# A new hand-written issue order for an adaptive-LayerNorm block on one core

## The chip, the core and the metric

The kernel runs on one core of a Trainium2 chip. The metric is the device time of one execution in microseconds (us). Three runs of the kernel before took 236.52, 236.69 and 236.73 us. TensorE (PE) multiplies matrices, VectorE (DVE) and ScalarE (ACT) work on elements, GpSimd (POOL) does a few small things, and SyncE (SP) issues nearly all the DMA transfers. PEld in the profile is TensorE's loading of weights.

## The reference

One token sequence x of 2048 x 512 passes through a transformer block whose two normalisations are scaled and shifted by a condition c:

```python
mod = (silu(c) @ w_mod).reshape(1, 6, 1, 512)
sa, ca, ga, sb, cb, gb = (mod[:, i] for i in range(6))
h = layernorm(x) * (1 + ca) + sa
x = x + ga * attention(h)
h = layernorm(x) * (1 + cb) + sb
x = x + gb * ((gelu(h @ w_gate) * (h @ w_up)) @ w_down)
```

The attention has 32 heads of width 16. Query s sees 8 keys only, those at s, s-2, ..., s-14, and the softmax runs over these 8. w_gate and w_up are 512 x 1792, w_down is 1792 x 512. All is bfloat16.

## The kernel before

**Segments and stages.** The 2048 tokens are four segments (sg 0 to 3) of 512. Each one passes through the same stages, and the stages of different segments are interleaved. The names below are those of the code; a number behind a name is the segment, a second one the part of it.

| stage of segment g | engine and line | what it does |
|---|---|---|
| LN1.g.st, vd, va, rs, x | DVE L430, L460, L465; POOL L471; DVE L448 | statistics by 128 rows, 1/deviation, xn = normalised x (four instructions x0 to x3) |
| LN1.g.sa, nm, sq | ACT L408, L414, L419 | the statistics of some rows on ACT instead |
| LN1.g.th (g = 0), LN1.1.t | PE L509, L484 | transposes of xn |
| LN1.g.t (g = 2, 3), LN2.g.t (g = 1, 2, 3) | SP L490 | the same as a DMA transpose |
| LN1.g.h | ACT L545, DVE L543 (g = 0); ACT or POOL L527, L525 | scale and shift: hT. For g = 0 these read the modulation mod01 |
| qph, qp.g.b.j | PE L580, L598 | q, k and v products (b = 0, 1, 2), four parts each; ACT (L618, L620, L624) copies them out |
| vst.g, V4.g.0 to 2, V4ld.g | SP L635, L644 | v goes to DRAM and comes back shifted, in four loads V; V4ld is the last of the four |
| pq.g.j, lp.g | DVE L664; PE L678 | q times the shifted k, then summed over a head by a column-tiled product |
| mx, z, e, s1, ri, p | DVE L695, L701, L711, L717, L722; ACT L706 | softmax |
| ptp.0; est, ptl (g > 0) | PE L736; SP L750, L758 | probabilities brought into v's layout |
| pv.g.j, o.g.j | DVE L771; PE L790 | probabilities times v, summed by a column-tiled product; ACT L801 copies out (oT) |
| x1p, x1, LN2 | PE L811; DVE L820; as LN1 | output projection, residual, second norm |
| g, u, gl, ub, hh | PE L844; ACT L878, L885; DVE L896 | gate and up products, gelu, their product: 14 tiles each |
| y, ot, sto | PE L856, L868; DVE L903; SP L928 | down product, residual, store |

The modulation needs products of its own: mp1 and mp0 (PE L348) for mod01 (DVE L355), mp3 and mp4 (PE L305), and mp2 and mp5 (PE L369) for ga and gb. gst and ga (SP L319, L323) send ga through DRAM to all partitions. At the head PE runs 20 products of zeros (w0 to w19, L217).

**Column-tiled products.** lp, o, ptp, mp2 and mp5 use only 32 columns of the array in an instruction and say which: `tile_position=(0, H * g)`. lp and o are eight instructions each, ptp, mp2 and mp5 sixteen. All other products use the full array. A run of column-tiled products with no full product between them is called a stretch here.

**The order.** Every stage is a Python generator (a thread) of operations. A list of thread numbers, ORDER, says which thread gives its next operation; this fixes the order of issue on each engine, and each engine's queue runs in that order:

```python
for i in ORDER:
    op = nxt[i]
    assert all(name in self.done for name in op.after), (op.fire, op.after)
    ...
    op.fn()
```

So an instruction that waits keeps back all that stands behind it on its engine. SP's queue is one too: a load that stands behind a store waits until that store has been issued. Buffers are few: one for vT (what ACT writes and vst sends), one for V, two for hT, four PSUM banks for the products q, k, v, g, u and y, and two for o and x1p.

Of the kernel before, what the change touches and what calls it, by code (L numbers as in the profile page):

```python
# [16 lines left out]
PT_DMA = (1, 2, 3)  # L17

ORDER = [
# [35 lines left out]
]  # L55


# [920 lines left out]
```

## Time and profile before

| | |
|---|---|
| runs | 236.52, 236.69, 236.73 us |
| span of the profiled execution | 234.1 us, so some 2.6 us of a run lie around it |
| TensorE's granted clock | 1.000 |
| PE busy | 230.0 us, 98% of the span |
| DVE, ACT, POOL busy | 170.4, 150.0, 18.6 us |
| DMA | 30.21 MB, mean 129 GB/s |

The page gives busy time by engine, a chain of what ended last, and groups of instructions. A row of the timeline has start, duration, engine, line, operation, output<-inputs and count; several instructions that follow one another are merged in a row. Matmuls are pipelined and overlap, so the distance from one start to the next is what counts, not the duration. An SP row says how long the issue took, not the transfer.

### The profile page before, as it was taken

To read this page: it belongs to the slowest core of one execution; us is meant where nothing else is said; L and a number is where in the kernel's file an instruction comes from. 1 tells how busy PE (TensorE), PEld (TensorE's weight loads), DVE (VectorE), ACT (ScalarE), POOL (GpSimd) and SP (SyncE) were. 2 spreads that over 40 slices of the span, in tenths; PEclk is the share of its full clock that TensorE was granted. 3 is DMA by queue.
4 is the path that set the end of the run, shared out by engine and by line. 5 is a ranking of instruction groups with operands and counts; after the bars stand their busy time and mean duration, and the time that the engine had idled before them with its cause. 6 is when DMAs were issued, how large, how long until landed. Compare 5 with 4: busy or idle time off the path is not lost.

```text
span 234.1 us, 3675 instructions
## 1 busy us (share of the span) xinstructions
PE 230.0 (98%) x1387; PEld 108.2 (46%) x1387; DVE 170.4 (73%) x240; ACT 150.0 (64%) x283; POOL 18.6 (8%) x43
## 2 busy tenths in 40 slices
PE   7999999999999999999999999999999999999995
PEld 2755455434644444444444444444444444444443
DVE  3999999999997999999799788467747421222222
ACT  4899997976997758936656492546754343666400
POOL 2612461000100000100000010000001000000000
PEclk9999999999999999999999999999999999999999
DMA  6997989999969839553102963510000411000011
GB/s 218 373 364 213 202 213 171 276 391 303 176 152 236 291 92 200 98 114 103 56 0 57 202 109 60 156 56 0 0 4 0 90 45 45 3 0 0 0 48 45
DMA packets 36265, 30.21 MB, mean 129 GB/s; under 512 B 14872, under 2 KB 34328, under 8 KB 36248
## 3 DMA queue, kind: packets, MB, share of 16 engines
q1 hardware_dynamic: 35968, 29.72, 50.6%
q10 hardware_dynamic: 280, 0.26, 0.3%
q8 instruction: 11, 0.18, 0.3%
q14 instruction: 6, 0.05, 0.1%
HBM read 22.37 MB, written 4.98 MB: 117 GB/s over the span
## 4 chain that ended last, share of the span: by engine, by line
PE 98%; DVE 0%; issue 0%
PE g_ps L844 21%; PE u_ps L844 21%; PE y_ps L856 19%; PE qkv_ps L598 17%; PE x_ps L811 6%; PE o_ps L790 3%; PE LTp L678 3%; PE warm_ps L217 3%; PE y_ps L868 1%; PE qkv_ps L580 1%; PE hTp L484 1%; PE hTp L509 0%; PE modT_ps L305 0%; PE modT_ps L348 0%; PE gR_ps L369 0%; PE PTp L736 0%
## 5 line engine op out<-in xcount | busy, mean ns | idle before, releaser
L844 PE MATMUL g_ps<-h,Wg 128*128 128x512 bf16 x224 | 57.5, 379 | 0.0
L844 PE MATMUL u_ps<-h,Wu 128*128 128x512 bf16 x224 | 57.5, 379 | 0.0
L878 ACT ACTIVATE gl<-g_ps 128x512 bf16<-128x512 f32 x56 | 33.6, 600 | 24.8 <-PE g_ps L844 23.9
L856 PE MATMUL y_ps<-Wd,hht 128*128 128x512 bf16 x210 | 46.0, 379 | 0.0
L885 ACT CAST ub<-u_ps 128x512 bf16<-128x512 f32 x56 | 32.8, 586 | 18.3 <-PE u_ps L844 18.1
L598 PE MATMUL qkv_ps<-hT,wqkv 128*128 128x512 bf16 x184 | 42.1, 380 | 0.0
L896 DVE TENSOR_TENSOR hht<-gl,ub 128x512 bf16<-128x512 bf16 x56 | 23.0, 421 | 25.3 <-ACT ub L885 25.0
L664 DVE TENSOR_TENSOR pq<-qT,kT 128x4096 bf16<-128x4096 bf16 x16 | 36.3, 2292 | 0.0
L771 DVE TENSOR_TENSOR pv<-PT,V 128x4096 bf16<-128x4096 bf16 x16 | 36.0, 2286 | 0.0
L844 PEld LDWEIGHTS <-Wg 128*128 128x128 bf16 x224 | 21.5, 98 | 27.3 <-issue 2.1
L844 PEld LDWEIGHTS <-Wu 128*128 128x128 bf16 x224 | 21.8, 98 | 26.6 <-issue 0.4
L856 PEld LDWEIGHTS <-hht 128*128 128x128 bf16 x210 | 20.5, 98 | 24.8
L598 PEld LDWEIGHTS <-wqkv 128*128 128x128 bf16 x184 | 20.1, 114 | 19.7 <-issue 3.0
L903 DVE TENSOR_TENSOR ot<-y_ps,x 128x512 bf16<-128x512 f32 x15 | 10.3, 689 | 20.2 <-PE y_ps L856 17.2
L471 POOL TENSOR_TENSOR rstd<-rstd,neghalf 128x4 f32<-128x4 f32 (+1 forms) x9 | 8.8, 980 | 154.1 <-DVE rstd L460 85.5
L527 ACT ACTIVATE h<-h,modT,scl 128x512 bf16<-128x512 bf16 x12 | 8.8, 802 | 11.6 <-DMA h<-xn 11.6
L811 PE MATMUL x_ps<-woP,oT 128*128 128x512 bf16 x64 | 15.3, 379 | 0.0
L430 DVE BATCH_NORM_STATS2 st<-x 128x6 f32<-128x512 bf16 x19 | 12.9, 680 | 3.1 <-DMA x<-in_A_x_dram 2.9
L820 DVE TENSOR_TENSOR x<-x_ps,x 128x512 bf16<-128x512 f32 x16 | 10.8, 686 | 5.0 <-PE x_ps L811 5.0
L801 ACT CAST oT<-o_ps 128x512 bf16<-128x512 f32 x16 | 8.9, 592 | 2.7 <-PE o_ps L790 2.7
L618 ACT CAST qT<-qkv_ps 128x512 bf16<-128x512 f32 x16 | 9.2, 587 | 2.2 <-PE qkv_ps L598 2.1
L620 ACT CAST kT<-qkv_ps 128x512 bf16<-128x512 f32 x16 | 9.5, 596 | 1.2 <-PE qkv_ps L598 1.2
(85 smaller groups left out, 181.5 us busy)
## 6 DMA issues: line engine op xcount, KB each, us to landing
V<-vscr SPq DMA_DIRECT2D x12, 520.0 KB, 10.4
wm<-in_w_mod_dram SPq DMA_DIRECT2D x6, 512.0 KB, 5.4
vscr<-vT SPq DMA_DIRECT2D x4, 512.0 KB, 4.2
out_dram<-ot SPq DMA_DIRECT2D x15, 128.0 KB, 1.7
Wg<-in_B_w_gate_dram SPq DMA_DIRECT2D x1, 1792.0 KB, 11.0
Wu<-in_B_w_up_dram SPq DMA_DIRECT2D x1, 1792.0 KB
wqkv<-in_A_wqkv_dram SPq DMA_DIRECT2D x3, 512.0 KB, 8.3
x<-in_A_x_dram SPq DMA_DIRECT2D x3, 512.0 KB, 8.6
```

The costliest lines, as they stand in the source:

```text
L430: nc.vector.bn_stats(out=st[:], in_=src()[:, c4, :])
L598: nc.tensor.matmul(ps[:], lhsT=wqkv[blk][:, dt, j::4], rhs=B["hT", sg][:, :, dt, :], start=(dt == 0), stop=(dt == DT - 1))
L664: nc.vector.tensor_tensor(out=pq[:], in0=_ap(B["qT", sg][:, j, :], [[0, W], [1, SG]]), in1=_ap(kT[:, j, sg % 3 * SG + 2:sg % 3 * SG + 2 + ...
L771: nc.vector.tensor_tensor(out=t[:], in0=_ap(B["PT", sg][:, 0, :], [[SG, 2], [0, 4], [1, SG]]), in1=_ap(v[:, 0, j, :], [[8, 2], [4 * (SG + ...
L811: nc.tensor.matmul(ps[:], lhsT=B["oT", sg][:, j, c4::CPS] if sg else B["oT", sg][:, j, c4 * P:(c4 + 1) * P], rhs=woP[:, j, :], start=(j == ...
L820: nc.vector.tensor_tensor(out=x[:, c4, :], in0=B["x1ps", sg, c4][:], in1=x[:, c4, :], op=ALU.add)
L844: nc.tensor.matmul(ps[:], lhsT=Wt[:, dt, ft * P:(ft + 1) * P], rhs=B["h2T", sg][:, :, dt, :], start=(dt == 0), stop=(dt == DT - 1))
L856: nc.tensor.matmul(ps[:], lhsT=B["hh", sg, ft][:, c4 * P:(c4 + 1) * P], rhs=B["Wd", ft // 4][:, ft % 4, :], start=(ft == 0), stop=(ft == F ...
L878: nc.scalar.activation(out=gl[:], in_=B["g", sg, ft][:], func=ACT.Gelu_apprx_tanh)
L885: nc.scalar.copy(out=ub[:], in_=B["u", sg, ft][:])
L896: nc.vector.tensor_tensor(out=hh[:], in0=B["gl", sg, ft][:], in1=B["ub", sg, ft][:], op=ALU.mult)
L903: nc.vector.tensor_tensor(out=ot[:], in0=B["y", sg, c4][:], in1=B["x", sg][:, c4, :], op=ALU.add)
```

## The change

Only ORDER is replaced. It holds the same 853 operations, and each thread's own sequence stays. Its first and last lines, of 41:

```diff
 ORDER = [
-    23, 23, 23, 23, 23, 23, 23, 23, 23, 23, 23, 2, 0, 0, 23, 1, 1, 22, 2, 31, 31, 31, 33, 22, 23, 22, 33, 33,
-    33, 33, 33, 33, 34, 34, 33, 34, 34, 23, 23, 22, 23, 23, 22, 35, 2, 22, 23, 35, 22, 36, 36, 24, 23, 23, 23,
-    3, 30, 30, 30, 37, 37, 37, 30, 30, 37, 36, 37, 6, 57, 57, 4, 59, 59, 57, 59, 59, 59, 7, 85, 85, 37, 37, 37,
...
-    131, 133, 131, 134, 131, 131, 133, 134, 133, 134, 133, 134,
+    23, 23, 23, 23, 23, 23, 23, 23, 23, 2, 0, 1, 0, 1, 22, 31, 31, 31, 6, 33, 2, 33, 23, 23, 23, 23, 23, 23, 23,
+    23, 33, 33, 33, 33, 33, 57, 59, 22, 34, 34, 2, 33, 59, 57, 34, 22, 23, 23, 22, 3, 57, 34, 7, 24, 22, 35, 22,
+    0, 23, 23, 4, 22, 35, 36, 36, 36, 30, 37, 30, 30, 83, 37, 37, 30, 30, 59, 9, 59, 59, 59, 83, 85, 8, 5, 37,
...
+    134, 131, 131, 133, 134, 131, 133, 134, 131, 133, 134,
 ]
```

Read out by engine, it means this. PE's stretches:

```
before, 15: mp2 | lp.0.0 | lp.0.1 lp.0.2 lp.0 | ptp.0 lp.1.0 | lp.1.1 o.0.0 lp.1.2 | o.0.1 | o.0.2 | o.0.3 | lp.1 |
            o.1.0 mp5 o.1.1 | o.1.2 o.1.3 | lp.2.0 lp.2.1 lp.2.2 lp.2 | o.2.0 lp.3.0 lp.3.1 lp.3.2 o.2.1 |
            o.2.2 o.2.3 lp.3 | o.3.0 o.3.1 o.3.2 o.3.3
after, 10:  lp.0.0 mp2 lp.0.1 | lp.0.2 lp.0 | ptp.0 lp.1.0 lp.1.1 | o.0.0 o.0.1 mp5 lp.1.2 o.0.2 o.0.3 | lp.1 |
            lp.2.0 lp.2.1 o.1.0 | o.1.1 lp.2.2 lp.2 o.1.2 o.1.3 | lp.3.0 lp.3.1 lp.3.2 |
            o.2.0 o.2.1 lp.3 o.2.2 o.2.3 | o.3.0 o.3.1 o.3.2 o.3.3
```

SP, up to the last V load of segment 0:

```
before: x0.0 wm1 wm0 wqkv0 x1 wqkv1 x2 wqkv2 wm2 wm3 x3 wo2 wo0 wo3 wo1 vst.0 LN1.2.t V4.0.0 gst2 V4.0.1 ga vst.1 V4.0.2 V4ld.0 LN1.3.t
after:  x0.0 x1 wm1 wm0 wqkv0 x2 wqkv1 wo0 x3 wqkv2 wm3 wo3 wo1 wm2 wo2 vst.0 LN1.2.t gst2 V4.0.0 V4.0.1 vst.1 V4.0.2 V4ld.0 LN1.3.t
```

DVE, up to pv.0.0:

```
before: LN1.0: st0 st1 vd0 st2 vd2 va2 x0 x1 x2 x3 | mod01 | LN1.0: h2.0 h3.0 h1.1 h2.1 h3.1 | LN1.1: st0 st1 st2 vd0 va0 |
        LN1.2.st0 LN1.2.st1 pq.0.0 LN1.2.st2 vd0 va0 | LN1.1: x0 x1 x2 x3 | LN1.2: x0 x1 x2 x3 | pq.0.1 pq.0.2 pq.0.3 pq.1.0 |
        lm.0 mx.0 z.0 pq.1.1 LN1.3.va0 s1.0 LN1.3: x0 x1 x2 x3 | ri.0 p.0 pq.1.2 pv.0.0
after:  LN1.0: st0 st1 vd0 st2 vd2 va2 | LN1.1.st0 | LN1.0: x0 x1 | LN1.1.st1 | LN1.0: x2 x3 | mod01 | LN1.0: h2.0 h3.0 h1.1 h2.1 h3.1 |
        LN1.1: st2 vd0 va0 | LN1.2: st0 st1 st2 vd0 va0 | LN1.1: x0 x1 x2 x3 | pq.0.0 LN1.2: x0 x1 x2 | pq.0.1 LN1.2.x3 |
        pq.0.2 pq.0.3 pq.1.0 | lm.0 mx.0 LN1.3.va0 z.0 LN1.3: x0 x1 x2 | s1.0 ri.0 p.0 LN1.3.x3 pq.1.1 pq.1.2 pv.0.0
```

ACT's order moves with these: LN1.1.sa3, nm and sq3 stand before the first evictions LN1.0.h0.0, h1.0 and h0.1 instead of behind them, and scB stands before these three instead of among them. POOL does LN1.3.rs between LN1.2.h0 and LN1.2.h1. On PE, qp.3.1.0 stands behind o.0.3 instead of ahead of it, and mp5 ahead of it; lp.3.0 to lp.3.2 follow y.0 directly; o.3 and x1p.3 stand between the parts of y.1 and g.2; and g.3.0 to u.3.2 stand between the parts of y.2. On ACT, sa and sq of LN2.1 stand around gl.0.11 to ub.0.13, so that the last sq follows ub.0.13. The instructions themselves, tiles and buffers do not change.

62 rows, old and new, of the table ORDER are left out of this document.

## The prediction, made before the result was known

> **What bounds the kernel now.** The page comes first: span, busy time, and the chain of what ended last.
>
> ```profile
> span 234.1 us, 3675 instructions
> ...
> PE 230.0 (98%) x1387; PEld 108.2 (46%) x1387; DVE 170.4 (73%) x240; ACT 150.0 (64%) x283; POOL 18.6 (8%) x43
> ...
> PE 98%; DVE 0%; issue 0%
> ```
>
> The chain that ended last is TensorE for 98% of its length. So a saving has to be a saving of PE's own time, and any other engine matters only where it makes PE late. The change removes no instruction; it can save only what lies between products. The timeline of PE shows one such place, a stretch of three column-tiled pieces (o.2.0, lp.3.0 to lp.3.2, o.2.1) between gate and up products:
>
> ```profile
> 118.20 1.03 PE L844 MATMUL g_ps<-h,Wg 128*128 128x512 bf16 x4
> 119.06 1.03 PE L844 MATMUL u_ps<-h,Wu 128*128 128x512 bf16 x4
> 120.02 0.62 PE L790 MATMUL o_ps<-pv,Msum 128*32 128x512 bf16 x8
> 120.46 1.47 PE L678 MATMUL LTp<-pq,Mph 128*32 128x512 bf16 x24
> 121.75 0.60 PE L790 MATMUL o_ps<-pv,Msum 128*32 128x512 bf16 x8
> 122.29 1.04 PE L844 MATMUL g_ps<-h,Wg 128*128 128x512 bf16 x4
> ```
>
> Read it from start to start. Four full products take 119.06 - 118.20 = 0.86 us, 0.215 each. The last four before the stretch take 120.02 - 119.06 = 0.96: entering costs 0.10. Inside, 24 column-tiled products take 1.29, so eight take 0.43; the first eight take 0.44, the last eight, up to the next full product, 0.54: leaving costs 0.11. With 0.01 to 0.02 in the first full group behind, a stretch costs about 0.23 us, however many pieces it holds.
>
> **The saving.** Ten stretches for fifteen: 5 x 0.23 = **-1.16 us** (0.2 to 0.25 each: -1.0 to -1.25). The products themselves number the same.
>
> **The head.** Three views of the timeline before the first full-size product, by engine: DVE, ACT, PE.
>
> ```profile
> 7.01 0.73 DVE L448 TENSOR_SCALAR xn<-x,mv,rstd 128x512 bf16<-128x512 bf16 x2
> 8.01 0.41 DVE L448 TENSOR_SCALAR xn<-x,mv,rstd 128x512 bf16<-128x512 bf16 x1 [0.27 <-POOL rstd L471]
> 8.34 0.41 DVE L448 TENSOR_SCALAR xn<-x,sums,rstd 128x512 bf16<-128x512 bf16 x1
> 8.78 0.17 DVE L355 TENSOR_TENSOR mod<-modT_ps,c 128x8 f32<-128x8 f32 x1
> 8.98 1.68 DVE L543 TENSOR_SCALAR hT<-hTp,mod 128x256 bf16<-128x256 bf16 x5
> 10.58 0.69 DVE L430 BATCH_NORM_STATS2 st<-x 128x6 f32<-128x512 bf16 x1
> ...
> 11.40 0.66 DVE L430 BATCH_NORM_STATS2 st<-x 128x6 f32<-128x512 bf16 x1
> ```
> ```profile
> 8.98 1.02 ACT L545 ACTIVATE hT<-hTp,mod 128x256 bf16<-128x256 bf16 x2 [0.82 <-DVE mod L355]
> ...
> 10.08 0.57 ACT L545 ACTIVATE hT<-hTp,mod 128x256 bf16<-128x256 bf16 x1
> ```
> ```profile
> 9.91 2.02 PE L580 MATMUL qkv_ps<-hT,wqkv 128*128 128x256 bf16 x16
> ...
> 11.76 1.46 PE L598 MATMUL qkv_ps<-hT,wqkv 128*128 128x512 bf16 x6
> ```
>
> A statistics step costs DVE 11.40 - 10.58 = 0.82 us, a normalisation 8.34 - 8.01 = 0.33. The new order puts LN1.1.st0 at 7.01 and LN1.1.st1 behind x1: x0 7.83, x1 8.16, st1 8.49, x2 9.31, x3 9.64, mod01 9.97 at the latest, less some hundredths where overlap is better. The evictions, 0.20 behind mod01's start, begin at about 10.15 instead of 8.98. The idle 0.27 in the second row is used up, which is why two steps of 0.82 cost 1.17 and not 1.64.
>
> ACT then does h0.0, h1.0 and h0.1 without scB between: 10.15, 10.61, 11.07, the last ending 0.57 later at 11.64. The fifth pair of half-width products (qph.1.0) needs h0.1; four pairs at (11.76 - 9.91) / 8 = 0.23 or a little less bring the first full product to about 12.55 instead of 11.76: **+0.79 us**. PE has nothing else there; the zero products run in either order. Below, the cover PE has (it started qph at 9.91, not waiting for h0.1) leaves perhaps +0.5. Above stands the load of x1, now issued ahead of wm1 and wm0. It takes wm1's place in the queue:
>
> ```profile
> L245 SPq DMA_DIRECT2D wm<-in_w_mod_dram x2: 453/480/507, 1.3 to 1.8; - x2
> ...
> DMA to landing us min/median/max: 4.6/4.6/4.6
> ```
>
> 1.3 + 4.6 = 5.9, before DVE needs it at 7.01. wm1 and wm0, one load later, have until 9.9. If x1's transfer slows what is still in flight of x0 or c by 0.4 to 0.7, the head is +1.5 at most.
>
> **The V loads of segment 0.** SP issues in order, and the order is new: LN1.2.t, then gst2, then the V loads. LN1.2.t needs all of LN1.2.x, and LN1.2.x3 now stands behind pq.0.1 on DVE. The rows of DVE, SP and the last V load (its 506 KB are the second of the pair at 31.54, so issued at about 32.2):
>
> ```profile
> 19.10 0.41 DVE L448 TENSOR_SCALAR xn<-x,sums,rstd 128x512 bf16<-128x512 bf16 x1
> 19.59 1.06 DVE L448 TENSOR_SCALAR xn<-x,mv,rstd 128x512 bf16<-128x512 bf16 x3
> 20.56 0.41 DVE L448 TENSOR_SCALAR xn<-x,sums,rstd 128x512 bf16<-128x512 bf16 x1
> 20.88 8.89 DVE L664 TENSOR_TENSOR pq<-qT,kT 128x4096 bf16<-128x4096 bf16 x4
> ...
> 41.68 8.90 DVE L771 TENSOR_TENSOR pv<-PT,V 128x4096 bf16<-128x4096 bf16 x4
> ```
> ```profile
> 21.09 3.42 SPq L490 DMA_TRANSPOSE hT<-xn  x1
> 24.61 0.62 SPq L644 DMA_DIRECT2D V<-vscr  x1
> 25.32 0.61 SPq L319 DMA_DIRECT2D gscr<-gR  x1
> ...
> 31.54 1.72 SPq L644 DMA_DIRECT2D V<-vscr  x2
> ```
> ```profile
> V<-vscr SPq DMA_DIRECT2D x1, 506.0 KB, 9.2
> ```
>
> DVE does the same set of work up to there without three small idles (0.27 at x2, 8.78 - 8.67 = 0.11 at mod01, 19.59 - 19.43 = 0.16): it is some 0.6 us ahead. One pq takes 2.20 in the queue (8.89 for four, overlapped). So LN1.2.x3 ends at 20.97 + 2.20 - 0.6 = 22.6, the transpose is issued at about 22.65, holds SP for 3.42 to 26.1, gst2 takes 0.65, and V4.0.0 goes out at about 26.75 instead of 24.61: +2.15.
>
> How much of that reaches the last load? The DMA engines' share by window decides:
>
> ```profile
> 31.50:33.00 1.50, 1.50 (x9) 0.78 (x8) 1.50 (x2) 1.50 (x6) 1.17 (x2) 1.00 0.62 169
> 33.00:37.00 4.00, 4.00 (x20) 2.13 (x19) 4.00 (x7) 2.93 (x6) 1.01 (x1) 1.00 1.04 254
> 37.00:41.40 4.40, 4.40 (x41) 2.17 (x39) 4.37 (x5) 3.68 (x8) 0.00 (x0) 1.00 1.23 147
> ```
>
> The seventh number behind the window is PEclk, the eighth the DMA share. From 33 to 41.4 the queue is full, so a load that enters late leaves late; only 1.5 x 0.38 = 0.57 us are free between 31.5 and 33. The delay at the landing of V4ld.0 lies between 0 (the loads of before were themselves held by vst.1, issued 30.90) and 2.15 - 0.57 = 1.6. I take **+1.15**, nearer to the upper end because the queue shows so little slack: landing before 32.21 + 9.16 = 41.37, after about 42.5.
>
> Four pv take 8.90, from 42.55 to about 51.45, so o.0.3 can start at about 51.5. When would PE come there by its own sum?
>
> ```profile
> 50.86 0.62 PE L790 MATMUL o_ps<-pv,Msum 128*32 128x512 bf16 x8
> ```
>
> 50.86, less 0.86 (qp.3.1.0, four full products, now behind it), plus 0.22 for mp5 ahead of it, plus 0.79 (head), less 4 x 0.23 (stretches saved by then): 50.08. So PE waits about **1.4 us**. That wait holds in it two smaller ones earlier on PE, for pq.1.1 (moved behind ri.0 and p.0) and for ACT behind LN1.3.h, which delay the same products and not others. Queued behind o.0.3 is qp.3.1.0 and all else of PE; the wait is paid in full unless PE itself is later.
>
> POOL is on this path too:
>
> ```profile
> L525 POOL TENSOR_SCALAR hT<-hT,mod x4: 767/768/3802, 26.6 to 31.9; 128x512 bf16<-128x512 bf16 x4
> ```
>
> Alone a scaling takes 0.77 us; the longest, from 26.62 to 30.42, lay beside the last two pq and took 3.80, so one of the two engines held the other back, there POOL. In the new order LN1.2.h1 starts right ahead of LN1.3.x0, and DVE could lose up to 0.75 us to it. Under the V loads' wait that disappears, and the sum is without it; where the loads land early it counts. The Trainium skill, page "SBUF — State Buffer", section "Who interferes with whom", says that a DVE instruction with two SBUF inputs and a GpSimd instruction that reads SBUF exclude each other for a whole instruction, whoever comes first. By that rule the 3.80 us are a wait for two pq, with which the row agrees, and the 0.75 us are as likely DVE's loss as POOL's.
>
> **Later waits.** In the second half the last statistics square of LN2.1 follows ub.0.13 on ACT instead of standing before it. The rows of y.0, the transpose and the scaling:
>
> ```profile
> 97.48 12.25 PE L856 MATMUL y_ps<-Wd,hht 128*128 128x512 bf16 x56
> ...
> 99.75 2.02 SPq L490 DMA_TRANSPOSE h<-xn  x1
> ...
> 104.23 2.93 ACT L527 ACTIVATE h<-h,modT,scl 128x512 bf16<-128x512 bf16 x4 [2.36 <-DMA h<-xn]
> ```
>
> From issue to the scaling 104.23 - 99.75 = 4.5 us, the scaling 2.93. By my replay of the new order, xn of LN2.1 is complete 6.4 us after the start of y.0, so g.1.0 could start 13.9 us after it; PE, with y.0 and the lp.3 pieces behind it, comes there after 13.6: +0.3. Some 0.15 more for x1p behind a late softmax, and 0 to 0.2 where o.0.2 of the residual holds a PSUM bank under g.1. I take **+0.5** (0 to +0.8). Stage by stage the other edges of the new order keep a margin; the tightest is o.1.0, with 0.05 us.
>
> **The sum.** -1.16 + 0.79 + 1.4 + 0.5 = +1.5 us: the span goes from 234.1 to about 235.6. The profiled execution has 2.6 us around its span if it stood at the median of the runs, 236.69, as I take it to: **238.2 us**.
>
> **Rivals.**
>
> *The V loads land as before* (41.4 us). For it: the stores vst.1 and the window of share 0.62. Against it: 6.9 us of full queue before the landing. DVE then reaches pv.0.0 by its own work at 41.68 - 0.6 = 41.1, pv.0.3 ends at 50.0, o.0.3 starts 0.3 later (as 50.57 to 50.86 before): PE waits 0.2. 236.69 - 1.16 + 0.79 + 0.2 + 0.5 = 237.0; with POOL in DVE's way for another 0.2 to 0.75, up to 237.5.
>
> *PE's own sum decides everywhere*: no wait at o.0.3, none later. Its place is V4ld.0; its point is a landing before about 41 us, with DVE in pv.0.0 by then, as it would be if a late V4.0.0 drew the four loads together and filled the gap of share 0.62. Then 236.69 - 1.16 + 0.79 = 236.3, with the head's lower end 236.0, with a stretch at 0.25 us and no wait at mod01 235.7. Not slower than before. Against it: the queue's share of 1.0 and more from 33 us on.
>
> *The head is dearer.* x1's transfer runs beside x0's rest and c: xn starts 0.4 to 0.7 later, all of it on PE's path, and V4 comes out later by as much: 238.2 + 0.5 + 0.5 = 239.2, up to 240. Against it: x1 is one load among several in a queue whose first loads took 4.6 us each with wm in the same place.
>
> That the change does not do what it says is excluded: the list, read out, has ten stretches.
>
> **How the numbers follow.** Forecast 0.47 (237.5 to 239.0); V loads as before 0.18 (236.7 to 237.5); PE's sum alone 0.19 (235.5 to 236.7); dearer head 0.16 (239.0 to 240.2). A measurement of this kernel tells about 0.2%, 0.47 us, from no change: under 236.22 is faster, over 237.16 slower. Faster: 0.15 of the third case. Same: 0.04 of it and 0.11 of the second. Slower: 0.07 of the second, the forecast and the fourth, 0.70. The range leaves out the lowest third of the third case (0.07) and the upper part of the fourth (0.11): 235.9 to 239.6.
>
> **What would show it.** Stretches: PE's row before each next full product should still have entry 0.10 and exit 0.11, and there should be ten; if the products around are dearer in a mixed stretch of o, mp5 and lp, -1.16 shrinks. Head: the L543 row at about 10.15 and the first L598 row at about 12.55. V loads: V4.0.0 issued at about 26.75, pv.0.0 at about 42.5, and PE idle ahead of o.0.3 or of a product in the 4 us before it, together 1.4. Later: up to 0.3 of idle ahead of g.1.0. The forecast is wrong if pv.0.0 starts before 41.5, or if the first L598 product starts before 12.2 or after 13.0.

## The result, and the profile after

The changed kernel takes 238.6 us (median of six runs, 237.64 to 239.68); the kernel before took 236.77 us beside it (236.52 to 237.68). The ratio is 1.007, interval 1.0046 to 1.0095: slower by 0.5 to 1.0%. The forecast was 238.2 us in a range of 235.9 to 239.6. The profiled execution is the slowest of the six, 239.68 us, with a span of 237.5. A second profile of the same kernel, taken for the first experiment, has 238.33 us and a span of 236.1, and stands beside it below where the two differ. In both 2.2 us lie around the span, and 2.2 to 2.3 in the later runs whose spans were compared; the span of 234.1 us of the kernel before thus belongs to an execution of about 236.3 us (an estimate), not to the median of 236.69.

The page of the changed kernel, the same three lines as in the prediction:

```profile
span 237.5 us, 3656 instructions
...
PE 229.7 (97%) x1376; PEld 108.9 (46%) x1387; DVE 170.8 (72%) x240; ACT 150.9 (64%) x283; POOL 16.4 (7%) x43
...
PE 81%; DMA 6%; DVE 5%; ACT 5%; issue 2%; POOL 0%
```

TensorE's busy time has not grown (eleven of its 1387 records are missing in this trace). The chain has changed: 98% of it was PE before, now 19% of what ended last lies on transfers and other engines. The waits of TensorE say where (total, times, longest, in us):

```profile
PE g_ps L844 <- ACT kT L620: 1.3, 1, 1.3
PE warm_ps L217 <- DVE gB L212: 1.2, 1, 1.2
PE LTp L678 <- DVE pq L664: 0.7, 1, 0.7
PE qkv_ps L598 <- DMA wqkv<-in_A_wqkv_dram: 0.6, 1, 0.6
PE modT_ps L348 <- DMA wm<-in_w_mod_dram: 0.5, 1, 0.5
```

Before, only the second row was there. The first is put down to ACT, which had ended at 69.16. Wg landed at 69.14, and the load of the first weights from it began at 69.18 with the product; in the second profile, where ACT's copy ends after that product has begun, the wait bears the name of Wg. So the wait is for the landing of Wg, though in the first profile ACT was no earlier. Now the head, DVE and then PE:

```profile
9.60 0.42 DVE L448 TENSOR_SCALAR xn<-x,sums,rstd 128x512 bf16<-128x512 bf16 x1
10.33 0.17 DVE L355 TENSOR_TENSOR mod<-modT_ps,c 128x8 f32<-128x8 f32 x1 [0.31 <-PE modT_ps L348]
```
```profile
9.75 0.55 PE L348 MATMUL modT_ps<-scT,wm 128*128 128x1 bf16 x16 [0.50 <-DMA wm<-in_w_mod_dram]
...
13.00 1.03 PE L598 MATMUL qkv_ps<-hT,wqkv 128*128 128x512 bf16 x4
14.63 2.57 PE L598 MATMUL qkv_ps<-hT,wqkv 128*128 128x512 bf16 x11 [0.60 <-DMA wqkv<-in_A_wqkv_dram]
```

The normalisation LN1.0.x3 begins at 9.60 (forecast 9.64), so the statistics cost VectorE what was counted. But mod01 then waits another 0.31 for mp0, and mp0 waited for wm0: the first full product comes at 13.00, not 12.55. In the second profile mp0 is done at 9.82, mod01 follows VectorE's own queue at 10.12 without idle, and the first full product comes at 12.70. The second group comes at 14.63, 1.63 behind the first instead of 0.86 (14.01, 1.31 behind, in the second profile), because wqkv1 is now behind x2. From issue to landing wm1 took 4.6 us before (the landing of wm0 is not in that trace). Now, with x1 ahead of both:

```profile
L245 SPq DMA_DIRECT2D wm<-in_w_mod_dram x2: 433/470/508, 1.8 to 2.3; - x2
...
DMA to landing us min/median/max: 6.4/6.9/7.4
```

wm0 landed at 2.29 + 7.41 = 9.70. In the second profile it took 6.9 and landed at 9.2, and the first full product came 0.3 us earlier. The changed kernel's scatter (2.0 us over six runs) is wider than that of before (1.2). The two profiles differ by 1.35 us, of which 0.3 lie at the first full product, 0.3 at the second group and 0.7 at g.0.0: all three are waits for loads, in one profile or in both.

The V loads, on SP, and the last of them (506 KB) among the DMA issues:

```profile
22.82 0.63 SPq L635 DMA_DIRECT2D vscr<-vT  x1
23.56 3.39 SPq L490 DMA_TRANSPOSE hT<-xn  x1
27.05 0.62 SPq L319 DMA_DIRECT2D gscr<-gR  x1
27.77 1.31 SPq L644 DMA_DIRECT2D V<-vscr  x2
...
52.63 1.54 SPq L223 DMA_DIRECT2D Wg<-in_B_w_gate_dram  x1
```
```profile
V<-vscr SPq DMA_DIRECT2D x1, 506.0 KB, 9.0
```

V4ld.0 (issued at 33.44) landed at 42.4, as forecast (42.5). Yet it did not set the start of pv.0.0. VectorE and POOL around it:

```profile
32.59 2.44 DVE L448 TENSOR_SCALAR xn<-x,sums,rstd 128x512 bf16<-128x512 bf16 x3
34.96 1.21 DVE L711 TENSOR_REDUCE ssum<-LTp 128x128 f32<-128x1024 f32 x1
...
38.65 4.49 DVE L664 TENSOR_TENSOR pq<-qT,kT 128x4096 bf16<-128x4096 bf16 x2
43.05 8.89 DVE L771 TENSOR_TENSOR pv<-PT,V 128x4096 bf16<-128x4096 bf16 x4
```
```profile
31.55 1.01 POOL L471 TENSOR_TENSOR rstd<-rstd,neghalf 128x4 f32<-128x4 f32 x1 [0.97 <-DVE rstd L465]
32.55 2.34 POOL L525 TENSOR_SCALAR hT<-hT,mod 128x512 bf16<-128x512 bf16 x3
```

VectorE has no idle time ahead of pv.0.0. Three normalisations of LN1.3 take 34.96 - 32.59 = 2.37 us, 0.79 each, where one took 0.33; they lie exactly beside POOL's three scalings, 32.55 to 34.89. So pq.1.1, the first of the pair at 38.65, ended at 40.93, and pv.0.0 started at 43.05. TensorE from lp.1.0 to o.0.3:

```profile
39.64 0.60 PE L678 MATMUL LTp<-pq,Mph 128*32 128x512 bf16 x8
40.98 0.62 PE L678 MATMUL LTp<-pq,Mph 128*32 128x512 bf16 x8 [0.73 <-DVE pq L664]
...
51.81 1.04 PE L790 MATMUL o_ps<-pv,Msum 128*32 128x512 bf16 x16
52.78 0.41 PE L598 MATMUL qkv_ps<-hT,wqkv 128*128 128x512 bf16 x1
```

TensorE waits at lp.1.1, which starts 0.05 behind the end of pq.1.1. From there to o.0.3 it has no wait: o.0.2 starts at 51.81 and o.0.3 0.43 later, at 52.25, when pv.0.3 had been done for 0.31 us (51.94). In the second profile lp.1.1 starts at 40.36, o.0.3 at 51.62, again 0.31 behind pv.0.3. In the new order lp.1.1 stands directly behind lp.1.0, seven full groups earlier than before, while pq.1.1 stands behind p.0 and LN1.3.x3 on VectorE. This is where VectorE's delay reaches TensorE.

The stretch o.2.0 to o.2.3 with lp.3, which was two before:

```profile
123.07 1.03 PE L844 MATMUL g_ps<-h,Wg 128*128 128x512 bf16 x4
124.03 1.05 PE L790 MATMUL o_ps<-pv,Msum 128*32 128x512 bf16 x16
124.90 0.60 PE L678 MATMUL LTp<-pq,Mph 128*32 128x512 bf16 x8
125.33 1.10 PE L790 MATMUL o_ps<-pv,Msum 128*32 128x512 bf16 x16
126.36 0.82 PE L844 MATMUL u_ps<-h,Wu 128*128 128x512 bf16 x3
```

Entry 0.96 - 0.86 = 0.10, 16 products 0.87, eight 0.43; the last 16 with the exit 1.03, which is 0.87 + 0.16. The price of entering and leaving is that of before, with some 0.05 more in this last part.

### The profile page after: what moved, and what is told of

Its sections match the earlier page's. It is cut to its first block, busy times and chain, and to the rows that moved or that the text cites. A ratio compares the mean times of both kernels' runs of the same rounds, so it can differ in the third digit from the quotient of the medians.

```text
span 237.5 us, 3656 instructions
## 1 busy us (share of the span) xinstructions
PE 229.7 (97%) x1376; PEld 108.9 (46%) x1387; DVE 170.8 (72%) x240; ACT 150.9 (64%) x283; POOL 16.4 (7%) x43
## 4 chain that ended last, share of the span: by engine, by line
PE 81%; DMA 6%; DVE 5%; ACT 5%; issue 2%; POOL 0%
PE g_ps L844 21%; PE u_ps L844 21%; PE y_ps L856 19%; PE qkv_ps L598 8%; PE x_ps L811 6%; DMA wqkv<-in_A_wqkv_dram 4%; PE o_ps L790 3%; PE LTp L678 2%; DVE pq L664 2%; DMA x<-in_A_x_dram 2%; PE y_ps L868 1%; DVE xn L448 1%; ACT h L527 1%; ACT hT L527 1%; ACT kT L620 1%
## 5 line engine op out<-in xcount | busy, mean ns | idle before, releaser
L598 PE MATMUL qkv_ps<-hT,wqkv 128*128 128x512 bf16 x184 | 41.7, 380 | 0.6 <-DMA wqkv<-in_A_wqkv_dram 0.6
L624 ACT CAST vT<-qkv_ps 128x512 bf16<-128x512 f32 x16 | 9.1, 592 | 2.0 <-PE qkv_ps L598 2.0
L811 PEld LDWEIGHTS <-oT 128*128 128x128 bf16 x64 | 6.9, 110 | 7.1 <-issue 0.4
## 6 DMA issues: line engine op xcount, KB each, us to landing
Wg<-in_B_w_gate_dram SPq DMA_DIRECT2D x1, 1792.0 KB, 16.5
```

Source lines behind the costliest of these rows:

```text
L598: nc.tensor.matmul(ps[:], lhsT=wqkv[blk][:, dt, j::4], rhs=B["hT", sg][:, :, dt, :], start=(dt == 0), stop=(dt == DT - 1))
L811: nc.tensor.matmul(ps[:], lhsT=B["oT", sg][:, j, c4::CPS] if sg else B["oT", sg][:, j, c4 * P:(c4 + 1) * P], rhs=woP[:, j, :], start=(j == ...
```

## The experiments

Twelve kernels ran, each timed against the kernel before on the same chip. The moves are given by engine; the list of thread numbers was rewritten to give them. Where a ratio stands, it is to the kernel before.

**again: the changed kernel once more.** No edit.

> The changed kernel once more, for its own scatter and a second profile. Three waits of TensorE stand in its first profile that the prediction did not price as such: 1.0 us at the second group of the first full products (wqkv1 landed at 14.58), 1.0 us at lp.1.1 (pq.1.1) and 1.5 us at g.0.0 (Wg landed at 69.14). If they are made by the order alone, this profile has the same three within 0.2 us. If they hang on how the transfers run this time, the one at g.0.0 differs by 0.5 us or more between the two profiles, as the scatter of the runs (237.64 to 239.68) makes likely. Time 238.2 to 239.0.

Measured: 238.32 us (237.56 to 239.26), ratio 1.0069 (1.0051 to 1.0088). Waits in its profile:

```profile
PE modT_ps L344 <- DMA wm<-in_w_mod_dram: 0.9, 1, 0.9
PE LTp L674 <- DVE pq L660: 0.7, 1, 0.7
PE g_ps L840 <- DMA Wg<-in_B_w_gate_dram: 0.6, 1, 0.6
```

The wait at lp.1.1 is the same, that at g.0.0 is 0.6 instead of 1.3, now under the name of Wg, which landed at 67.79 and not at 69.14. The wait for wqkv1 is 0.3 instead of 0.6. So the order makes the wait at lp.1.1, while those at the head and at g.0.0 move with the transfers. (Line numbers are four lower here.)

**wg: Wg earlier.**

```diff
 SP:
-  vst.2  V4.1.0  Wg  V4.1.1
+  vst.2  Wg  V4.1.0  V4.1.1
```

> Only the load of Wg is moved on SP: right behind vst.2 instead of behind V4.1.0, which waits until pv.0.3 has freed V. Theory Wg (the load sets the start of g.0.0): the wait at g.0.0 goes, 0.5 to 1.5 us less than the changed kernel, about 237.5. Theory of the prediction (Wg is early enough, all delay was made before o.0.3): no difference, within 0.3 us of the changed kernel.

Measured: 238.32 us (237.74 to 239.08), ratio 1.0079 (1.0065 to 1.0094). In the profile Wg landed at 61.1, the wait at g.0.0 is gone, and g.0.0 started at 67.01 instead of 67.83; the execution with this profile took 237.74 us. But the medians of the two kernels are equal. So Wg is late in the profiles, by 0.6 to 1.3 us; that its place costs time over many runs is not shown.

**x3: LN1.2.x3 ahead of pq.0.1.**

```diff
 DVE:
-  LN1.2.x2  pq.0.1  LN1.2.x3  pq.0.2
+  LN1.2.x2  LN1.2.x3  pq.0.1  pq.0.2
```

> Only LN1.2.x3 is moved on VectorE, ahead of pq.0.1 as in the kernel before; so LN1.2.t and the V loads are issued about 2.2 us earlier, and POOL's scalings h0 to h3 too. Theory V loads (the prediction): V4ld.0 lands 1 to 1.6 us earlier than 42.4, pv.0.0 starts with it, o.0.3 about 1.2 us earlier, about 237.4. Theory VectorE queue: pv.0.0 starts when VectorE has done what stands ahead of it; POOL no longer lies beside LN1.3.x0 to x2 (0.33 instead of 0.80 us each), lp.1.1's wait is shorter, pv.0.0 starts 1.0 us earlier; about 237.6. What tells them apart is whether VectorE is idle ahead of pv.0.0. If Wg alone decides and does not come earlier with pv.0.3: no change.

Measured: 238.30 us (237.77 to 239.62), ratio 1.0078 (1.0056 to 1.0100): no difference, and neither theory was put to the test, since LN1.2.t did not move. SP in this profile:

```profile
22.94 0.64 SPq L631 DMA_DIRECT2D vscr<-vT  x1
23.69 3.49 SPq L486 DMA_TRANSPOSE hT<-xn  x1
```

LN1.2.x3 ended at 20.8, but LN1.2.t was still issued at 23.69, right behind vst.0. vst.0 waits until ScalarE has copied the last v tile. Here ScalarE began that copy at 22.33, 0.04 behind TensorE's last v product and with no idle time ahead of it, so that both are late together: TensorE by the head and by LN1.1.t0, which now stands ahead of the v products; ScalarE by LN1.1.h0, LN1.1.h1 and LN1.3.sa1, which now stand ahead of or among its v copies. The step "LN1.2.t is issued when LN1.2.x3 is done" was wrong: the store ahead of it on SP is what holds it.

**head: x1 and wqkv1, two statistics steps and ScalarE's first work put back as before.**

```diff
 SP:
-  x0.0  x1  wm1  wm0  wqkv0  x2  wqkv1
+  x0.0  wm1  wm0  wqkv0  x1  wqkv1  x2
 DVE:
-  LN1.1.st0  LN1.0.x0  LN1.0.x1  LN1.1.st1  LN1.0.x2 ... LN1.0.h3.1
+  LN1.0.x0  LN1.0.x1  LN1.0.x2 ... LN1.0.h3.1  LN1.1.st0  LN1.1.st1
 ACT:
-  LN1.1.sa3  LN1.1.nm  ...  LN1.1.sq3  scB  LN1.0.h0.0  LN1.0.h1.0  LN1.0.h0.1
+  ...  scB  LN1.0.h0.0  LN1.0.h1.0  LN1.0.h0.1  LN1.1.sa3  LN1.1.nm  LN1.1.sq3
```

> The head of the kernel before inside the new list: x1 behind wqkv0 and wqkv1 behind x1 on SP, LN1.1.st0 and st1 behind the evictions of LN1.0 on VectorE, LN1.1.sa3, nm and sq3 behind the first evictions on ScalarE. The first full product should start at about 11.7 instead of 12.9, and the 1.0 us wait for wqkv1 should go. If delays of TensorE add up: 1.2 to 2.2 us less than the changed kernel, about 236.9. If o.0.3 is pinned by pv.0.3, as the prediction has it, nothing of that arrives: TensorE waits at o.0.3 instead, and the time is within 0.3 us of the changed kernel.

Measured: 239.71 us (239.18 to 240.15), ratio 1.0128 (1.0110 to 1.0146): slower than the changed kernel. The first full product came at 11.94, 0.8 to 1.1 us earlier than there. Then TensorE waited 1.9 us for ScalarE, which stood behind LN1.2.sa3, and that waited for x2, now landed at 14.2. And VectorE, which had lost what it had won at the head, started pv.0.0 at 44.04; TensorE waited 1.5 us at lp.1.1, and o.0.3 came at 53.24. An earlier TensorE was worth nothing, and a later VectorE cost time.

**bx1: the kernel before with x1 first.**

```diff
 SP (before):
-  x0.0  wm1  wm0  wqkv0  x1  wqkv1
+  x0.0  x1  wm1  wm0  wqkv0  wqkv1
```

> The kernel before with one load moved on SP: x1 ahead of wm1 and wm0 instead of behind wqkv0. No statistics are moved. Theory load (the head of the changed kernel is late because wm0 lands late behind x1): wm0 lands at 9.2 to 9.7 instead of under 8.2, mod01 starts at about 9.6 to 10.1 instead of 8.78, the first full product at 12.2 to 12.8 instead of 11.76, and as TensorE waits for nothing later, the time is 0.5 to 1.0 us above before: 237.2 to 237.6, with more scatter than before. Theory statistics (the prediction: VectorE's two statistics steps make the head late): no difference from before, 236.6.

Measured: 237.78 us (237.25 to 237.97), ratio 1.0038 (1.0026 to 1.0049): 0.9 us over before, with no statistics moved. TensorE's head:

```profile
9.67 0.55 PE L344 MATMUL modT_ps<-scT,wm 128*128 128x1 bf16 x16 [0.48 <-DMA wm<-in_w_mod_dram]
...
13.24 1.03 PE L594 MATMUL qkv_ps<-hT,wqkv 128*128 128x512 bf16 x4
```

The load alone moves the first full product from 11.76 to 13.24. So the statistics are not needed for the head's delay; whether they would make it alone, this run can't say.

**hdve: only the two statistics steps back.**

```diff
 DVE:
-  LN1.1.st0  LN1.0.x0  LN1.0.x1  LN1.1.st1  LN1.0.x2 ... LN1.0.h3.1
+  LN1.0.x0  LN1.0.x1  LN1.0.x2 ... LN1.0.h3.1  LN1.1.st0  LN1.1.st1
```

> The changed kernel with LN1.1.st0 and st1 back behind the evictions of LN1.0 on VectorE, as in the kernel before; loads and ScalarE as in the changed kernel. Theory statistics (the prediction: these two steps make the first full product late, +0.79): it starts 0.8 us earlier and the time falls by up to 0.8 us, to 237.6. Theory load (wm0's landing at 9.2 to 9.7 makes it late, and the two steps fill time in which VectorE would only wait for it): the first full product stays at 12.5 to 12.9, VectorE loses about 1.2 us in its queue, pv.0.0 and o.0.3 come 1.0 to 1.4 us later, and the time rises to about 239.5.

Measured: 239.19 us (238.94 to 239.37), ratio 1.0105 (1.0089 to 1.0121): 0.9 us slower than the changed kernel. VectorE's head:

```profile
8.38 0.41 DVE L444 TENSOR_SCALAR xn<-x,sums,rstd 128x512 bf16<-128x512 bf16 x1
9.69 0.17 DVE L351 TENSOR_TENSOR mod<-modT_ps,c 128x8 f32<-128x8 f32 x1 [0.91 <-PE modT_ps L344]
```

VectorE now stands idle 0.91 us for wm0's product, the first full product is at 12.70, as in the second profile of the changed kernel (12.70), and pv.0.0 comes at 43.67. But mod01 starts at 9.69, 0.4 to 0.6 us earlier than there, and TensorE gains nothing by it: ScalarE, which now does LN1.1.sq3 and scB ahead of the first evictions, begins these at 10.32 without idle time. So three walls stand close together at the head of the changed kernel, and which one is last differs between the runs: wm0's product, VectorE's queue with the two steps, and ScalarE's queue. The two moved steps cost TensorE nothing here: they fill a wait, and the lead that they give VectorE is needed at lp.1.1 (41.61 here) and o.0.3 (52.87).

**pshort: POOL's scalings cut to a quarter.** This kernel scales 128 of 512 columns in LN1.2.h0 to h3 and leaves the others unscaled.

```diff
-  nc.gpsimd.tensor_scalar(out=o, in0=o, ...)
+  nc.gpsimd.tensor_scalar(out=o[:, 0], in0=o[:, 0], ...)
```

> The changed kernel with POOL's four scalings of LN1.2 cut to the first 128 of their 512 columns (the other columns keep the unscaled xn, so this kernel leaves out part of the computation). Everything else stands. If POOL holds VectorE back: LN1.3.x0 to x2 take 0.33 us each instead of 0.80, s1.0 waits for e.0 instead (so 1.0 us are won, not 1.4), lp.1.1's wait goes, pv.0.0 starts with V4ld.0's landing at 41.7 or so, 0.7 us earlier, and with it V4.1.0, Wg and g.0.0: 0.5 to 0.8 us less than the changed kernel, about 237.7. If the 0.80 us had another cause: no difference.

Measured: 237.78 us (236.52 to 238.64), ratio 1.0035 (1.0019 to 1.0051): 0.5 to 0.8 us under the two medians of the changed kernel, nearly half of the loss; the two intervals just touch (the changed kernel once more has 1.0051 to 1.0088). VectorE:

```profile
31.82 1.48 DVE L448 TENSOR_SCALAR xn<-x,sums,rstd 128x512 bf16<-128x512 bf16 x3
33.22 1.21 DVE L711 TENSOR_REDUCE ssum<-LTp 128x128 f32<-128x1024 f32 x1
...
41.80 8.90 DVE L771 TENSOR_TENSOR pv<-PT,V 128x4096 bf16<-128x4096 bf16 x4 [0.41 <-DMA V<-vscr]
```

The three normalisations take 1.40 us instead of 2.37, the wait at lp.1.1 is gone, and now VectorE does wait for the V load, 0.41 us. This is the wait that the forecast had for VectorE; it stood behind another one. o.0.3 comes at 50.80, as early as before (50.86), and yet 0.9 us of loss are left in the medians. An estimate from the rows finds part of it: ahead of o.0.3 the new order has 0.86 us of products less (qp.3.1.0) and 0.22 more (mp5), so that 0.64 us more are left to do from the same moment on, less 0.23 for the stretch saved behind it.

**psgst: the same, and gst2 behind V4.0.0.** POOL's scalings are cut as in pshort.

```diff
 SP:
-  LN1.2.t  gst2  V4.0.0  V4.0.1
+  LN1.2.t  V4.0.0  gst2  V4.0.1
```

> POOL's four scalings cut to a quarter as in the earlier run (part of LN1.2 stays unscaled, so this kernel leaves out part of the computation), and in addition gst2 behind V4.0.0 on SP as in the kernel before. In the run with short scalings VectorE stood idle 0.41 us ahead of pv.0.0 until V4ld.0 had landed at 41.73. Theory that the V loads are the next wall: V4.0.0 goes out 0.65 us earlier, V4ld.0 lands 0.3 to 0.65 earlier, the idle goes, pv.0.0 starts at 41.4, the time is 0.3 to 0.4 us below that run, 237.2 to 237.5. Theory that the transfers are held by vst.1 and not by the order of issue: V4ld.0 lands at 41.7 again, no difference.

Measured: 237.46 us (236.69 to 240.18), ratio 1.0042 (1.0018 to 1.0066). V4.0.0 went out at 26.42 instead of 27.03, V4ld.0 landed at 41.35 instead of 41.73, and pv.0.0 started at 41.43 without idle. The trace agrees with the theory that the V loads are the second wall. In the time the step is too small: the intervals of pshort and psgst overlap, and the ratio is no lower.

**pre and prew: the first 139 operations of the list before, then the new list; in prew also Wg behind vst.2.** The diff is the join of the two lists: all up to the issue of LN1.2.t as before, the rest as after, still ten stretches.

> The first 139 operations of the list before (head, loads, statistics, v store, up to the issue of LN1.2.t), then the new list for all the rest: ten stretches, and gst2 still ahead of V4.0.0. The first full product is back at 11.7, V4.0.0 at about 25.3, pv.0.0 at about 41.9, so o.0.3 comes at about 50.9 instead of 51.4 to 52.0. If delay is only made up to o.0.3, then the time is 236.2 to 236.7, all of the loss gone. If Wg's place sets g.0.0: Wg is issued behind V4.1.0 at about 51.5 and lands 15 to 16.5 us later, at about 67, while TensorE would be there at 65.5, so about 1.5 us are lost again there: 237.7 to 238.2.

> As the kernel with the first 139 operations of before, and Wg right behind vst.2. Theory that two causes lie one behind the other (the head with what hangs on it, and Wg): no wait at g.0.0, 1.0 to 1.5 us less than without the move of Wg, about 236.5: equal to before, because the wait for pv.0.3 eats what the stretches save until there. If the stretches' saving arrives in full: 235.6.

Measured: pre 238.51 us (238.25 to 239.28), ratio 1.0071 (1.0053 to 1.0089); prew 238.80 us (238.45 to 239.31), ratio 1.0084 (1.0066 to 1.0102). prew lies 2.3 us above what was expected, pre above both of its theories. In prew's profile the first full product is back at 11.7, and V4.0.0 at 25.69, but LN1.3.x0 to x2 still take 2.36 us beside POOL, pv.0.0 starts at 43.17, and o.0.3 at 52.36. TensorE waits 2.7 us for pq in all, 1.4 of it at lp.1.1:

```profile
PE LTp L674 <- DVE pq L660: 2.7, 2, 1.4
```

POOL's collision does not come from the late head. It is built into the new order of POOL: LN1.3.rs, on which LN1.3.x0 waits, stands directly ahead of h1, h2 and h3, so both engines are let go at the same moment. The Wg question stays as it was: with o.0.3 at 52 nothing was left to tell in the times.

**split5: the kernel before with five stretches more.**

```diff
 PE (before):
-  g.0.11  u.0.11  lp.2.0  lp.2.1  lp.2.2  lp.2
+  lp.2.0  g.0.11  lp.2.1  u.0.11  lp.2.2  lp.2
-  u.2.6  g.2.7  u.2.7  o.3.0  o.3.1  o.3.2  o.3.3
+  o.3.0  u.2.6  o.3.1  g.2.7  o.3.2  u.2.7  o.3.3
```

> The kernel before with five more stretches and nothing else: o.3.0, o.3.1 and o.3.2 each behind another full group, lp.2.0 and lp.2.1 too, so 20 stretches for 15. At 0.23 us for a stretch: 1.15 us above before, 237.8 to 237.9. If what counts is the number of pieces and not of stretches: no difference from before. If a stretch costs more than the entry and exit that the profile shows, for instance 0.4 us: 238.6.

Measured: 237.89 us (237.69 to 238.11) beside 236.70, ratio 1.0049 (1.0034 to 1.0064): +1.19 us, 0.24 for a stretch (0.16 to 0.30 by the interval).

```profile
165.33 0.61 PE L786 MATMUL o_ps<-pv,Msum 128*32 128x512 bf16 x8
165.87 1.04 PE L840 MATMUL u_ps<-h,Wu 128*128 128x512 bf16 x4
166.84 0.62 PE L786 MATMUL o_ps<-pv,Msum 128*32 128x512 bf16 x8
167.39 1.04 PE L840 MATMUL g_ps<-h,Wg 128*128 128x512 bf16 x4
```

Each piece alone takes 0.54 to 0.55 with its exit, each full group 0.97 with its entry. So the price of a stretch read off the rows is also its price in the time, where TensorE is the bound.

**gab: the kernel before with two stretches fewer.**

```diff
 PE (before):
-  mp2  mp3  lp.0.0
+  mp3  mp2  lp.0.0
-  o.0.2  qp.3.0.0  qp.3.1.0  o.0.3
+  qp.3.0.0  qp.3.1.0  o.0.2  o.0.3
```

(ScalarE's copy of qp.3.1.0 moves with it, ahead of the copy of o.0.2.)

> The kernel before with two stretches fewer and nothing else: mp2 joined with lp.0.0, and o.0.2 held back to stand beside o.0.3, so 13 for 15. Each 0.23: 0.46 us less. But TensorE then comes to o.0.3 0.4 us earlier and has to wait about 0.2 us for pv.0.3, which ends at 50.57 either way. Theory that o.0.3 is pinned by pv.0.3: nothing is won up to there, o.0.3 stands at 50.8 as before, and the whole is 0.0 to 0.25 us less than before. Theory that a stretch saved is a stretch won: 0.46 us less, 236.2.

Measured: 236.69 us (236.11 to 237.29) beside 236.70, ratio 1.0000 (0.9990 to 1.0011). VectorE and TensorE at the place:

```profile
41.61 8.89 DVE L767 TENSOR_TENSOR pv<-PT,V 128x4096 bf16<-128x4096 bf16 x4
```
```profile
50.10 1.07 PE L786 MATMUL o_ps<-pv,Msum 128*32 128x512 bf16 x16
51.10 1.05 PE L594 MATMUL qkv_ps<-hT,wqkv 128*128 128x512 bf16 x4
```

pv.0.0 started at 41.61 (before 41.68) and pv.0.3 ended 8.89 later, at 50.50. o.0.2 begins at 50.10, the next full product at 51.10 instead of 51.41. So o.0.3 came 0.3 us earlier than before, at 50.55, which is 0.05 behind the end of pv.0.3, and could not have come earlier still. Of the 0.46 us that two stretches save ahead of that point, 0.3 arrive in the trace, 0.2 are left at the end of the span (233.9 for 234.1), and the time shows nothing; its interval allows 0.24. So already in the kernel before, TensorE and VectorE arrive at o.0.3 nearly together: TensorE shows no wait there, and yet it has only 0.3 us of room to come earlier. No kernel here beats the one before.

## Why the prediction was right, point by point

The time and its sign came out as forecast, 238.6 for 238.2, and so did the place where most of the first half's loss is made: VectorE comes late with its work for o.0.3. The sum's terms did less well than the sum, and part of the agreement is luck. The terms can be measured on TensorE from start to start. The second group is late by 14.63 - 13.00 less 0.86, lp.1.1 by 40.98 - 39.64 less 0.43, g.0.0 by 69.18 - 65.12 less the 2.59 of the twelve products ahead of it:

| term, us | forecast | first profile | second profile |
|---|---|---|---|
| five stretches (at the price of 0.23) | -1.16 | -1.16 | -1.16 |
| first full product | +0.79 | +1.24 | +0.94 |
| second group, behind wqkv1 | none | +0.77 | +0.45 |
| wait before o.0.3 (measured at lp.1.1) | +1.4 | +0.91 | +0.90 |
| later waits (measured at g.0.0) | +0.5 | +1.47 | +0.75 |
| sum | +1.5 | +3.2 | +1.9 |
| span against 234.1 | +1.5 | +3.4 | +2.0 |

So the sum was 0.5 us short even beside the faster of the two profiles. The 2.6 us that the forecast laid around the span made up for most of that: 2.2 was measured.

1. **Stretches, -1.16.** Right in price: 0.23 forecast, 0.24 by split5. Four of the five lie ahead of o.0.3, and gab shows for the kernel before that of a saving there at most about half arrives in the time. The prediction had this in its form, since it set the 1.4 us of wait against TensorE's shortened sum. In the changed kernel the joining itself makes a wait possible: with lp.1.1 drawn up to lp.1.0, TensorE asks for pq.1.1 before VectorE has it.

2. **Head, +0.79.** Half right. "mod01 9.97 at the latest" is what VectorE's queue allowed: it was free at 10.0 in the first profile, and mod01 started at 10.12 without idle in the second. What failed is that wm1 and wm0 "have until 9.9". wm0 landed at 9.2 to 9.7 behind x1, and mp0 (16 products, 0.55) and mod01 have to follow it; in the first profile this came 0.31 us behind VectorE. ScalarE's queue, which stood free at 10.32 in hdve, was a third wall that the prediction took for free. bx1 makes the delay by the load alone, in the kernel before, and hdve keeps it with the two steps gone: where one of the three is taken away, another holds TensorE. The first full product was late by 0.9 to 1.2, and the second group by a further 0.5 to 0.8 for wqkv1 behind x2, which the prediction passed over. At lp.1.1 TensorE waits for VectorE in both profiles, so that coming earlier from the head would win it nothing there. head and prew agree, though VectorE is late in them as well: first full product at 11.94 and 11.71, lp.1.1 at 41.97 and 41.10, where the second profile has 12.70 and 40.36.

3. **V loads and o.0.3, +1.4.** Forecast: V4.0.0 at 26.75, V4ld.0 landed at 42.5, pv.0.0 at 42.55, o.0.3 at 51.5. Measured in the two profiles: V4.0.0 27.77 and 27.18, landing 42.4 and 41.7, pv.0.0 43.05 and 42.42, o.0.3 52.25 and 51.62. The numbers are near and three steps are wrong.

   V4.0.0 is late behind vst.0 and not behind LN1.2.x3 (x3). Of its delay of 3.2 and 2.6 us, only 1.0 and 0.3 reached the landing, so that the landing in the first profile is right by chance.

   The sentence that failed most is "DVE then reaches pv.0.0 by its own work at 41.68 - 0.6 = 41.1": from LN1.3.x0 to x2 VectorE lost 1.4 us beside POOL, not the "up to 0.75" counted for h1 alone, and thus its own queue is 0.6 to 0.7 us later than the load. pshort takes most of POOL's work away and the forecast's own wait of VectorE appears, 0.41 us. The collision was left out of the sum as hidden, and it was the bound.

   And TensorE's idle time, expected "ahead of o.0.3 or of a product in the 4 us before it, together 1.4", is not there. It lies 11 us earlier, at lp.1.1, behind pq.1.1, and is 0.9; the prediction had named this wait, as a smaller one that the other holds in it. In hdve, head and prew too lp.1.1 starts 0.05 us behind the end of pq.1.1, and o.0.3 11.26 us later.

   The rule of the Trainium skill that was weighed in that place is stated for VectorE instructions with two SBUF inputs, and a normalisation reads one tensor. The Trainium skill, page "SBUF — State Buffer", section "Who interferes with whom", also says that a `tensor_scalar` can contend with GpSimd, when it runs in a mode that takes both of VectorE's ports. No run shows the mode. The trace agrees in that the two engines went in step, 0.79 us for each pair, and the last normalisation ended 0.14 us behind the last scaling (35.03 and 34.89). It doesn't show that they exclude each other for their whole length: a pair would then take 0.33 + 0.77 = 1.10 us.

4. **Later waits, +0.5.** The three that were priced (g.1.0, x1p.1, the bank under g.1) are not there: no wait of TensorE stands in the list behind g.0.0. One that was called safe is there instead. The remark "the tightest is o.1.0" overlooked Wg, moved from 42.30 to 52.63 on SP: it took 16.5 us to land, where it took 11.0 before, and g.0.0 was late by 0.7 to 1.5 us in the two profiles. The size of the term is thus right by chance; and over many runs wg did not show it.

The rivals: TensorE's own sum did not decide. The V loads landed as forecast in the first profile, but in the second at 41.7, nearer to the first rival's 41.4; that rival also had "POOL in DVE's way", with at most half of the loss that was measured. The head was dearer than its term, but not as the fourth case had it: xn started at 7.78, not later than counted.

## What to carry to other kernels

An engine at 98% without a wait can still be pinned: look where another engine's work ends within some tenths of a microsecond of the moment it is needed, for a saving ahead of that point is won only up to these tenths, and a delay of the other engine beyond them costs time. When an order is changed, add up the queue of every engine that feeds such a point, and ask what each release lets go at the same time on two engines that hinder each other. Drawing a product forward to save a switch also draws forward the moment at which its input is asked for. The first loads of this kernel behaved as one queue: with x1 put ahead, wm1 landed at 7.7 to 8.2 instead of 5.9.

## What the runs showed of the hardware

Three VectorE normalisations (128x512 bf16, 0.33 us each alone) beside three POOL scalings (0.77 alone) took 2.37 us for VectorE and 2.34 for POOL: POOL lost nothing, VectorE 1.4 us. A 512 KB load at the start of the kernel took 4.6 us from issue to landing as second on SP, 5.9 to 6.4 as third and 6.9 to 7.4 as fourth, and the landing of the fourth differed by 0.5 us between two executions of the same kernel (9.2 and 9.7).
